# Maxima and exponentials that read a PSUM group in any order, with a newly searched instruction order, in linear attention followed by a squared-ReLU layer

## The chip, the core and the metric

The kernel runs on one core of a Trainium2 chip. Time is device time of one execution in microseconds. The engines are TensorE (PE, matrix products into PSUM), VectorE (DVE), ScalarE (ACT), GpSimd (POOL, here almost only an issuer of loads) and SyncE (SP, an issuer of stores and of transposes by DMA). All run their own queues in order, and wait for each other by semaphores.

## The reference

Eight batches of eight heads, 576 tokens, head width 64, 128 features. Attention is linear, with positive and negative exponential features; its output, 4608 tokens of 512, goes through a two-layer network with a squared ReLU between.

```python
def phi(x):
    proj = np.einsum('bhsd,df->bhsf', x, w_phi)
    proj = proj - np.max(np.abs(proj), axis=-1, keepdims=True)
    return np.concatenate([np.exp(proj), np.exp(-proj)], axis=-1)
q_p, k_p = (phi(q), phi(k))
kv = np.einsum('bhsf,bhsd->bhfd', k_p, v)
z = np.sum(k_p, axis=2)
num = np.einsum('bhsf,bhfd->bhsd', q_p, kv)
den = np.einsum('bhsf,bhf->bhs', q_p, z)[..., None] + 1e-06
...
h = np.maximum(x @ w_in, 0.0)
return (h * h @ w_out).astype(np.float32)
```

## The kernel before, in words

The kernel first lists some 1738 small operations in the order of the mathematics (`plan.add`), each with its engine, and then issues them in another order, written out by hand as the table `ORDER`. `pin` chains every instruction behind the previous one of its engine, so `ORDER` fixes each engine's queue. Waits between engines are made from what each instruction reads and writes. The costs and the read and write lists given to `add` belong to the search that made the tables; at run time nothing comes from them but the operation's number.

Five tables go with it. `ORDER` is the order of issue. `BASES` gives each PSUM group one of the eight banks. `STATES` chooses ACT or DVE for each operation that may run on either (relu, output copies, KV copies, copies of PE transposes). `GATES` names for every load of batches 2 to 7 an operation that must be over before POOL may issue it. `FILL` puts products of a zero tile into PE's queue in the first microseconds.

One batch of attention goes like this. Queries and keys are turned so that the head width lies on the partitions: by PE and a copy in batches 0 and 1 (L316), by a DMA that SP issues in batches 2 to 7 (L326: one for K, one for Q). A projection (Pk, Pq; L342, or L369 and L494 in the first batch) puts 128 tokens by 128 features for up to four tiles and two heads into two PSUM banks. From these the keys get a maximum of absolute values on DVE (Mk, L397) and two exponentials on ACT (Ekp, Ekn, L403), not yet scaled. The maxima go through an exponential (em, L416 and L422) and scale the values instead (V, L430 on DVE). KV (L458, L463) is the product of key features and scaled values, copied to bf16 by ACT or DVE (L190, L192). For the queries of batches 0 to 3 the maximum (L501) and the features (Fq L572, exponentials L587) come from two products; from batch 4 on ("turned") one product gives a maximum (Mq, L534) and two exponentials (L547), and a DMA turns the features (Xf, L551). The numerators and denominators come from NA and NB (L651), with a scaling between them (L663) and a division after (L673, L677); a DMA turns the result (Xx, L711) into the layer's input xT.

The layer works on 512 tokens at a time, nine such chunks. F1 (L797, four 128x512 matmuls) makes 128 hidden units, relu (L774 on ACT or L776 on DVE) and square (L783 on DVE) follow; F2 (L891, four matmuls at a time) sums over the hidden units; an output copy (ot, L190 or L192) and a store end it. Matmuls of the layer for earlier chunks stand in PE's queue between the small products of the next batch's attention. The first chunk runs in smaller pieces (L808, L822, L836) so as to start early.

Where one PSUM group is read by a maximum and by two exponentials, the listing of before has each of them as a reader and a writer of the group, in the order maximum, positive exponential, negative exponential; the negative one closes the group. The first batch's keys use one bank for each head of a pair, and there the two banks are taken in opposite order by the two engines.

Of the kernel before, what the change touches and what calls it, by code (L numbers as in the profile page):

```python
# [20 lines left out]
def act_cost(n):  # L21
    return max(n / 1200 + 0.050, 0.105), n / 1200 + 0.165 + SEM


def dve_cost(n):
    return n / 960 + 0.064, n / 960 + 0.150 + SEM
# [27 lines left out]
class Plan:  # L54
# [6 lines left out]
    def add(self, eng, cost, fn, r=(), w=(), opens=None, closes=None, dma=None, tiled=False, release=False, what=""):  # L61
        op = Op(eng, cost, fn, opens, closes, dma, tiled, release, len(self.ops), what)
        before = {}
# [44 lines left out]
def kernel(  # L108
# [13 lines left out]
    Fd = w_phi.shape[1]  # L122
# [181 lines left out]
    def attention(b):  # L304
# [49 lines left out]
        def kgroup_ops(g):  # L354
# [7 lines left out]
            if first:  # L362
# [11 lines left out]
                def maxes(e, last):  # L374
                    def fn():
                        pin(nc.vector.tensor_reduce(
                            out=mk_view(g)[:, e, :], in_=ps1(pj[e])[:, : n * Fd].rearrange("p (i f) -> p i f", f=Fd),
                            axis=AX.X, op=ALU.max, apply_absolute_value=True))
                    add("DVE", dve_cost(n * Fd), fn, r=[pj[e]], w=[pj[e], ("mk", s2, g, e)],
                        closes=pj[e] if last else None, what="Mk")  # L380

                def exps(e, last):
                    for sgn, dst, nm in ((1.0, kp, "kp"), (-1.0, kn, "kn")):
                        def fn(dst=dst, sgn=sgn):
                            pin(nc.scalar.activation(out=dst[slot][:, e, :n, :].rearrange("p i f -> p (i f)"),
                                                     in_=ps1(pj[e])[:, : n * Fd], func=ACT.Exp, scale=sgn))
                        add("ACT", act_cost(n * Fd), fn, r=[pj[e]], w=[pj[e], (nm, slot, e)],
                            closes=pj[e] if last and sgn < 0 else None, what="E" + nm)

                maxes(0, False)  # L390
                exps(1, False)
                exps(0, True)
                maxes(1, True)
# [6 lines left out]
            add("DVE", dve_cost(2 * n * Fd), fn, r=[pj], w=[pj] + [("mk", s2, g, e) for e in range(2)], what="Mk")  # L400
            for sgn, dst, nm in ((1.0, kp, "kp"), (-1.0, kn, "kn")):
                def fn(dst=dst, sgn=sgn):
                    pin(nc.scalar.activation(out=dst[slot][:, :, :n, :].rearrange("p e i f -> p e (i f)"),  # L403
                                             in_=ps2(pj)[:, :, : n * Fd], func=ACT.Exp, scale=sgn))
                add("ACT", act_cost(2 * n * Fd), fn, r=[pj], w=[pj] + [(nm, slot, e) for e in range(2)],
                    closes=pj if sgn < 0 else None, what="E" + nm)
# [117 lines left out]
        def q_turned(c):  # L524
# [12 lines left out]
            add("DVE", dve_cost(2 * n * Fd), fn, r=[pj], w=[pj, ("mq", s2, c)], what="Mq")  # L537
            for sgn, base in ((1.0, 0), (-1.0, 2 * n * P)):
# [9 lines left out]
                add("ACT", act_cost(2 * n * Fd), fn, r=[pj], w=[pj, ("qf", f, sgn)], closes=pj if sgn < 0 else None,  # L548
# [422 lines left out]
    0, 1, 14, 11, 10, 9, 13, 4, 5, 2, 7, 3, 6, 12, 20, 85, 74, 15, 86, 50, 75, 87, 51, 18, 76, 88, 89, 52, 41, 54,  # L971
    19, 77, 78, 17, 42, 55, 79, 53, 16, 58, 80, 82, 63, 90, 27, 64, 56, 93, 81, 29, 65, 57, 8, 21, 112, 61, 66, 67,
    108, 36, 62, 113, 83, 106, 91, 101, 25, 43, 109, 68, 100, 110, 44, 45, 28, 84, 111, 71, 22, 59, 46, 107, 102, 47,
    116, 49, 60, 94, 69, 99, 31, 147, 103, 48, 117, 72, 24, 148, 144, 23, 145, 119, 73, 92, 26, 149, 96, 228, 234,
    95, 98, 70, 172, 97, 30, 229, 126, 173, 120, 38, 122, 222, 127, 105, 32, 123, 230, 223, 121, 124, 104, 231, 128,
    37, 125, 235, 216, 130, 118, 129, 146, 175, 232, 131, 217, 137, 132, 39, 138, 176, 133, 139, 134, 210, 140, 211,
    135, 177, 141, 150, 136, 151, 158, 233, 161, 35, 159, 152, 162, 142, 329, 153, 143, 236, 160, 154, 163, 204, 330,
    237, 325, 33, 205, 164, 331, 155, 333, 257, 156, 238, 326, 157, 165, 206, 341, 327, 207, 239, 34, 328, 166, 344,
    167, 174, 342, 168, 114, 178, 332, 40, 115, 334, 179, 212, 378, 335, 337, 213, 345, 180, 202, 214, 181, 347, 182,
    203, 346, 215, 383, 186, 336, 169, 338, 187, 348, 183, 170, 339, 200, 184, 190, 171, 224, 241, 188, 340, 189,  # L980
    350, 191, 185, 225, 201, 379, 192, 267, 382, 356, 351, 245, 268, 385, 243, 256, 193, 357, 353, 194, 226, 218,
    343, 377, 195, 242, 219, 354, 362, 227, 505, 355, 247, 220, 196, 509, 197, 240, 269, 259, 221, 580, 264, 298,
    244, 246, 513, 394, 248, 352, 299, 265, 387, 208, 359, 249, 363, 381, 258, 300, 517, 585, 358, 380, 250, 209,
    280, 198, 251, 388, 281, 260, 518, 384, 254, 349, 386, 368, 364, 360, 199, 575, 282, 252, 361, 261, 262, 369,
    253, 255, 289, 370, 263, 276, 270, 290, 277, 365, 271, 395, 291, 292, 523, 293, 272, 366, 283, 374, 266, 284,
    294, 375, 285, 527, 286, 295, 287, 519, 307, 296, 273, 288, 308, 531, 301, 396, 309, 371, 302, 274, 316, 303,
    317, 535, 372, 304, 376, 318, 310, 305, 559, 275, 579, 279, 536, 311, 306, 581, 397, 401, 367, 312, 398, 541,
    537, 313, 399, 314, 297, 545, 419, 400, 373, 402, 278, 319, 582, 418, 315, 409, 549, 410, 403, 553, 417, 320,
    411, 563, 321, 393, 412, 567, 322, 554, 390, 420, 571, 404, 323, 578, 389, 444, 572, 466, 445, 450, 467, 576,
    510, 583, 451, 514, 511, 574, 441, 512, 515, 528, 421, 392, 468, 442, 506, 773, 529, 577, 457, 507, 413, 458,  # L990
    405, 777, 516, 502, 414, 584, 459, 524, 391, 503, 434, 778, 415, 520, 424, 406, 592, 532, 416, 530, 546, 508,
    425, 407, 427, 560, 423, 426, 504, 525, 422, 542, 547, 428, 533, 526, 593, 550, 521, 433, 543, 548, 408, 564,
    522, 534, 544, 447, 565, 435, 429, 586, 561, 448, 573, 538, 774, 430, 555, 551, 589, 324, 431, 552, 449, 446,
    452, 436, 475, 432, 484, 476, 610, 539, 439, 443, 437, 477, 440, 611, 568, 438, 460, 569, 556, 612, 461, 702,
    613, 540, 462, 706, 557, 772, 463, 570, 485, 566, 590, 602, 464, 756, 974, 486, 603, 465, 469, 775, 760, 470,
    971, 604, 558, 453, 587, 471, 454, 710, 771, 472, 562, 456, 605, 473, 493, 784, 714, 494, 474, 594, 598, 715,
    595, 764, 495, 716, 599, 617, 596, 768, 597, 478, 600, 776, 638, 479, 720, 591, 639, 601, 588, 480, 724, 782,
    481, 640, 616, 482, 654, 781, 487, 620, 655, 483, 496, 977, 488, 728, 769, 489, 623, 732, 615, 455, 490, 656,
    491, 738, 497, 622, 492, 625, 663, 641, 664, 498, 770, 642, 742, 789, 665, 746, 499, 624, 500, 606, 644, 619,
    750, 607, 501, 703, 751, 608, 739, 645, 631, 630, 969, 704, 699, 614, 621, 609, 980, 733, 721, 618, 780, 734,  # L1000
    705, 626, 700, 752, 722, 972, 717, 646, 701, 627, 973, 723, 632, 783, 740, 647, 672, 718, 799, 779, 673, 711,
    648, 970, 707, 674, 787, 800, 725, 708, 709, 628, 801, 712, 785, 735, 726, 713, 1168, 633, 790, 629, 757, 802,
    968, 719, 741, 636, 736, 758, 657, 637, 650, 727, 681, 651, 729, 682, 658, 634, 643, 730, 659, 747, 731, 683,
    635, 660, 761, 661, 748, 986, 666, 975, 791, 690, 667, 899, 691, 749, 737, 668, 903, 669, 692, 979, 792, 765,
    670, 793, 759, 649, 983, 794, 803, 662, 743, 766, 804, 978, 675, 671, 744, 753, 676, 812, 805, 745, 917, 1366,
    762, 754, 788, 677, 767, 813, 907, 806, 1166, 678, 763, 679, 684, 811, 653, 1362, 795, 685, 680, 847, 921, 786,
    755, 796, 1363, 925, 976, 848, 911, 820, 797, 686, 819, 929, 912, 821, 798, 687, 935, 688, 849, 689, 807, 835,
    930, 939, 836, 850, 943, 822, 837, 851, 947, 817, 808, 838, 693, 953, 948, 809, 957, 931, 840, 810, 913, 918,
    839, 652, 852, 908, 828, 694, 695, 909, 900, 910, 896, 696, 987, 901, 697, 827, 1167, 902, 871, 859, 919, 872,
    961, 897, 926, 816, 873, 920, 860, 936, 1176, 814, 874, 1178, 904, 898, 937, 861, 965, 815, 818, 927, 862, 823,  # L1010
    829, 914, 966, 863, 932, 905, 915, 824, 916, 988, 883, 922, 989, 933, 906, 990, 698, 940, 884, 923, 991, 825,
    924, 984, 967, 938, 954, 949, 981, 830, 826, 941, 841, 1008, 955, 958, 942, 842, 885, 833, 1011, 959, 843, 928,
    834, 831, 875, 886, 934, 950, 844, 889, 832, 864, 845, 1004, 951, 960, 853, 1005, 944, 982, 846, 1114, 945, 854,
# [100 lines left out]
```

## Time and profile before

| what | value |
|---|---|
| median of 3 runs | 354.33 us (352.88 to 354.97) |
| the profiled execution | 353.94 us |
| its span in the trace | 352.2 us |
| PE, DVE, ACT, POOL busy | 341.5, 268.9, 233.3, 96.2 us |
| first transposes on PE | 5.7 us after the span's start |
| granted TensorE clock | 0.995 of full speed, mean |

A page of a profile gives for each engine the time in which at least one of its instructions ran. Of a group of instructions it gives the line, the engine, the tiles written and read with their shapes, the count, busy time, the mean duration of one in ns, and the idle time of the engine ahead of them with what ended it ("<-DVE mk L397" means that an instruction of line 397 on DVE released it). A matmul's duration runs until its result is out, and the next one begins earlier than that.

### The profile page before, as it was taken

The numbers are of one execution on the slowest core, as the hardware profiler recorded it, in microseconds if no ns is written. First come the engines' busy times: TensorE is split into PE (matmuls) and PEld (weight loads), VectorE is DVE, ScalarE is ACT, GpSimd is POOL, SyncE is SP. The second block draws the span as 40 slices with busy tenths as digits, with TensorE's granted clock in tenths as the row PEclk, the third lists the DMA queues.
The fourth block names the chain that finished last, engine by engine and source line by source line (L and its number), as shares of the span: only waits on it lengthen the run. The fifth ranks groups of instructions, "written<-read, shape, count | busy, mean of one in ns | idle before, by whom it ended". The sixth has DMA issues, their size and how long they took to land.

```text
span 352.2 us, 8392 instructions
## 1 busy us (share of the span) xinstructions
PE 341.5 (97%) x3343; PEld 192.0 (55%) x3343; DVE 268.9 (76%) x513; ACT 233.3 (66%) x439; POOL 96.2 (27%) x144
## 2 busy tenths in 40 slices
PE   6999999999999999999999999999999999999995
PEld 6778866544644555445545555455555554444443
DVE  4899997889887989689979887877989653564150
ACT  3999997789885776976597785895596503212111
POOL 8673461282461636021421302040100000000000
PEclk9999999999999999999999999999999999999999
DMA  8999999999999899997999999999857431100115
GB/s 92 172 196 202 201 155 168 159 122 167 162 130 189 138 150 151 165 201 152 163 140 202 165 212 140 214 106 179 155 117 157 96 87 67 60 2 0 71 50 120
DMA packets 133623, 49.05 MB, mean 139 GB/s; under 512 B 102096, under 2 KB 129104, under 8 KB 133584
## 3 DMA queue, kind: packets, MB, share of 16 engines
q0 software_dynamic: 45232, 18.36, 46.0%
q1 hardware_dynamic: 88112, 29.99, 44.3%
q8 instruction: 26, 0.43, 0.5%
q10 hardware_dynamic: 240, 0.16, 0.2%
q14 instruction: 13, 0.11, 0.1%
HBM read 36.77 MB, written 9.44 MB: 131 GB/s over the span
## 4 chain that ended last, share of the span: by engine, by line
PE 77%; DVE 10%; ACT 5%; DMA 5%; issue 2%; SPq 0%; DVEq 0%; ACTq 0%; POOLq 0%
PE psum L797 27%; PE psum L891 27%; PE psum L651 4%; PE psum L458 4%; PE psum L342 4%; PE psum L836 2%; DMA out_dram<-ot 2%; DVE va L430 2%; DMA xT<-xo 2%; DVE mk L397 1%; ACT hr L774 1%; DMA xk<-in_k_dram 1%; DVE hr L776 1%; PE psum L572 1%; DVE h L783 1%
## 5 line engine op out<-in xcount | busy, mean ns | idle before, releaser
L891 PE MATMUL psum<-wout,h 128*128 128x512 bf16 x560 | 134.9, 379 | 0.2 <-ACT ot L192 0.2
L797 PE MATMUL psum<-xT,win 128*128 128x512 bf16 x448 | 106.9, 379 | 1.4 <-DVE hr L776 0.8
L774 ACT ACTIVATE hr<-psum 128x512 bf16<-128x512 f32 x103 | 59.8, 596 | 54.5 <-PE psum L797 36.8
L891 PEld LDWEIGHTS <-h 128*128 128x128 bf16 x560 | 50.4, 97 | 54.6 <-issue 0.9
L797 PEld LDWEIGHTS <-win 128*128 128x128 bf16 x512 | 47.6, 97 | 54.3 <-issue 2.7
L783 DVE TENSOR_TENSOR h<-hr 128x512 bf16<-128x512 bf16 x144 | 56.6, 415 | 20.6 <-ACT hr L774 19.8
L547 ACT ACTIVATE qf<-psum 128x1024 bf16<-128x1024 f32 (+1 forms) x40 | 36.5, 938 | 12.3 <-DVE mq L534 11.3
L397 DVE TENSOR_REDUCE mk<-psum 128x8 f32<-128x1024 f32 (+1 forms) x35 | 38.6, 1110 | 4.6 <-PE psum L342 4.5
L587 ACT ACTIVATE qpn<-psum 128x1024 bf16<-128x1024 f32 (+1 forms) x40 | 36.7, 938 | 5.7 <-PE psum L572 4.9
L403 ACT ACTIVATE kp<-psum 128x1024 bf16<-128x1024 f32 (+1 forms) x35 | 32.7, 935 | 9.3 <-DVE mk L397 9.2
L651 PEld LDWEIGHTS <-qpn 128*128 128x128 bf16 x624 | 27.8, 98 | 13.9 <-issue 1.0
L663 DVE TENSOR_TENSOR psum<-psum,en 128x520 f32<-128x520 f32 (+1 forms) x39 | 27.2, 701 | 9.5 <-PE psum L651 5.6
L776 DVE TENSOR_SCALAR hr<-psum 128x512 bf16<-128x512 f32 x41 | 27.8, 685 | 6.7 <-PE psum L797 6.2
L403 ACT ACTIVATE kn<-psum 128x1024 bf16<-128x1024 f32 (+1 forms) x35 | 32.8, 937 | 0.0
L651 PE MATMUL psum<-kv,qpn 128*128 128x65 bf16 x624 | 31.1, 193 | 0.0
L430 DVE TENSOR_TENSOR va<-xv,va 64x256 bf16<-64x256 bf16 (+2 forms) x66 | 30.1, 471 | 0.9 <-ACT va L422 0.2
L245 POOL DMA_DIRECT2D xv<-in_v_dram x27 | 19.7, 734 | 36.0 <-DVE h L783 11.8
L245 POOL DMA_DIRECT2D xk<-in_k_dram x28 | 20.6, 740 | 31.6 <-ACT va L422 20.0
L677 DVE TENSOR_TENSOR xo<-psum,rden 128x512 bf16<-128x512 f32 (+1 forms) x39 | 26.7, 686 | 1.4 <-DMA xT<-xo 0.7
L265 POOL DMA_DIRECT2D xq<-in_q_dram x24 | 17.4, 725 | 33.0 <-ACT hr L774 13.7
L534 DVE TENSOR_REDUCE mq<-psum 128x8 f32<-128x1024 f32 (+1 forms) x20 | 22.3, 1113 | 2.9 <-PE psum L342 2.7
L501 DVE TENSOR_REDUCE mq<-psum 128x8 f32<-128x1024 f32 (+1 forms) x20 | 22.0, 1111 | 0.9 <-PE psum L342 0.8
(79 smaller groups left out, 383.5 us busy)
## 6 DMA issues: line engine op xcount, KB each, us to landing
out_dram<-ot SPq DMA_DIRECT2D x32, 256.0 KB, 3.1
xk<-in_k_dram POOLq DMA_DIRECT2D x26, 128.0 KB, 4.6
xq<-in_q_dram POOLq DMA_DIRECT2D x24, 128.0 KB, 4.8
xv<-in_v_dram POOLq DMA_DIRECT2D x24, 128.0 KB, 4.5
win<-in_moe_w_in_dram POOLq DMA_DIRECT2D x4, 512.0 KB, 9.2
wout<-in_moe_w_out_dram POOLq DMA_DIRECT2D x4, 512.0 KB, 14.0
xq<-in_q_dram POOLq DMA_DIRECT2D x4, 256.0 KB, 7.1
out_dram<-ot SPq DMA_DIRECT2D x6, 128.0 KB, 2.4
```

The source lines that it names most:

```text
L245: pin(nc.gpsimd.dma_start(out=x[:, a * 512 : z * 512].rearrange("p (h x) -> p h x", x=4 * D), in_=src[b][2 * a : 2 * z, 0:512, :].rearrang ...
L397: pin(nc.vector.tensor_reduce(out=mk_view(g), in_=ps2(pj)[:, :, : n * Fd].rearrange("p e (i f) -> p e i f", f=Fd), axis=AX.X, op=ALU.max, ...
L403: pin(nc.scalar.activation(out=dst[slot][:, :, :n, :].rearrange("p e i f -> p e (i f)"), in_=ps2(pj)[:, :, : n * Fd], func=ACT.Exp, scale= ...
L430: pin(nc.vector.tensor_tensor(out=t[:, :, :D].rearrange("p m (x c) -> p m x c", c=2), in0=x.rearrange("p (m x c) -> p m x c", m=n, c=2), i ...
L547: pin(nc.scalar.activation(out=o, in_=i_, func=ACT.Exp, scale=sgn))
L587: pin(nc.scalar.activation(out=o, in_=i_, func=ACT.Exp, scale=sgn))
L651: pin(nc.tensor.matmul(out=o[:, u // 4, u % 4 * D1 : (u % 4 + 1) * D1], lhsT=qpn[slot][:, sg * half + u * m : sg * half + u * m + P], rhs= ...
L774: pin(nc.scalar.activation(out=hr[sl], in_=ps1(g), func=ACT.Relu))
L776: pin(nc.vector.tensor_scalar(out=hr[sl], in0=ps1(g), scalar1=0.0, scalar2=None, op0=ALU.max))
L783: pin(nc.vector.tensor_tensor(out=dst, in0=i_, in1=i_, op=ALU.mult))
L797: pin(nc.tensor.matmul(out=o, lhsT=win[mc // 4][:, kc, mc % 4 * P : (mc % 4 + 1) * P], rhs=x, start=(kc == 0), stop=(kc == KC - 1)))
L891: pin(nc.tensor.matmul(out=ps1(g), lhsT=h2[c % 2][mc // 4][:, mc % 4, tt * P : (tt + 1) * P], rhs=wout[mc // 4][:, mc % 4, :], start=(mc = ...
```

## The change

In the listing, the maximum and the two exponentials of a projection are now readers of its group only, so that the search may put them in any of the six orders; a mark (`lock`) tells the search that they exclude each other. The closing of the group is no longer tied to the negative exponential. Then all five tables are new. Every operation has the same number as before, does the same on the same data, and there are as many.

```diff
-    def add(self, eng, cost, fn, r=(), w=(), opens=None, closes=None, dma=None, tiled=False, release=False, what=""):
+    def add(self, eng, cost, fn, r=(), w=(), opens=None, closes=None, dma=None, tiled=False, release=False, what="", lock=None):
         op = Op(eng, cost, fn, opens, closes, dma, tiled, release, len(self.ops), what)
+        op.lock = lock
...
-            add("DVE", dve_cost(2 * n * Fd), fn, r=[pj], w=[pj] + [("mk", s2, g, e) for e in range(2)], what="Mk")
+            add("DVE", dve_cost(2 * n * Fd), fn, r=[pj], w=[("mk", s2, g, e) for e in range(2)], lock=pj, what="Mk")
...
-                add("ACT", act_cost(2 * n * Fd), fn, r=[pj], w=[pj] + [(nm, slot, e) for e in range(2)],
-                    closes=pj if sgn < 0 else None, what="E" + nm)
+                add("ACT", act_cost(2 * n * Fd), fn, r=[pj], w=[(nm, slot, e) for e in range(2)], lock=pj, what="E" + nm)
...
-            add("DVE", dve_cost(2 * n * Fd), fn, r=[pj], w=[pj, ("mq", s2, c)], what="Mq")
+            add("DVE", dve_cost(2 * n * Fd), fn, r=[pj], w=[("mq", s2, c)], lock=pj, what="Mq")
...
 FILL = {
-    85: (0, 26), 87: (0, 4), 63: (7, 27), 65: (7, 10), 112: (7, 4), 108: (7, 3), 110: (7, 3), 116: (7, 23),
-    147: (0, 5), 144: (3, 5), 228: (5, 2), 139: (7, 7), 135: (7, 4),
+    74: (0, 26), 76: (0, 6), 87: (0, 3), 52: (7, 26), 63: (7, 6), 65: (7, 6), 116: (7, 26), 112: (7, 25),
 }
```

What the tables change, counted from them:

| | before | after |
|---|---|---|
| groups (without the first batch's keys) with one maximum and two exponentials: maximum first, between, last | 55, 0, 0 | 26, 13, 16 |
| relu on ACT, on DVE | 103, 41 | 109, 35 |
| output copies on ACT, on DVE | 20, 15 | 24, 11 |
| KV copies on ACT, on DVE | 22, 10 | 20, 12 |
| filler products | 123 | 124 |
| POOL's first loads, ahead of the mask (ident) | k, k, k, k, k | k, k, k, k, q |
| instructions of ACT ahead of the first relu | 50 | 49 |

The next table is about the DMA that turns K or Q of a batch (`Xxk`, `Xxq`): the PE operations that stand in `ORDER` between it and the first projection that reads it, for some of the twelve.

| transpose | before | after |
|---|---|---|
| K of batch 2 | 7 F2 or F1 pieces, 4 NA, 3 NB, 1 Pq, 2 Fq | 6 F2 or F1 pieces, 2 NA, 2 NB, 1 Pq, 2 Fq |
| K of batch 4 | 7 F1 or F2, 1 KV, 1 Pk, 2 Pq, 1 Fq | 6 F1 or F2, 1 KV, 1 Pq, 1 NA, 1 NB |
| Q of batch 7 | 9 F1 or F2, 1 KV, 1 Pk, 1 Pq, 3 NA, 3 NB | 5 F2, 3 NA, 3 NB |

All 1738 numbers of `ORDER`, the 385 banks, the 231 choices and the 108 gates differ in most places and are left out here.

## What was predicted

> **What bounds the kernel now.** First the page's busy table and slices, to see which engine the span belongs to.
>
> ```profile
> PE 341.5 (97%) x3343; PEld 192.0 (55%) x3343; DVE 268.9 (76%) x513; ACT 233.3 (66%) x439; POOL 96.2 (27%) x144
> ...
> PE   6999999999999999999999999999999999999995
> ...
> DVE  4899997889887989689979887877989653564150
> ACT  3999997789885776976597785895596503212111
> ```
>
> TensorE (PE) is busy in 341.5 of 352.2 us, and VectorE (DVE) and ScalarE (ACT) are dense only up to about slice 31. Next the busy time of each engine in four stretches: two of the start, the mixed middle, and the tail of feed-forward matmuls.
>
> ```profile
> 10.00:20.00 10.00, 9.03 (x123) 6.74 (x122) 8.85 (x19) 9.48 (x25) 5.44 (x9) 0.98 1.52 183
> 20.00:30.00 10.00, 9.88 (x189) 7.98 (x189) 9.94 (x24) 10.00 (x19) 6.41 (x9) 1.00 1.37 199
> ...
> 28.00:275.00 247.00, 243.83 (x2575) 137.12 (x2574) 214.88 (x393) 194.17 (x360) 75.57 (x112) 1.00 1.08 162
> 275.00:340.00 65.00, 65.00 (x360) 30.46 (x359) 30.72 (x67) 15.24 (x30) 0.00 (x0) 1.00 0.20 56
> ```
>
> The columns after the length are PE, weight loads, DVE, ACT and POOL. From 10 to 30 us ACT (19.5 of 20) and DVE (18.8 of 20) are full: the first batch's features are limited by them. From 275 us on PE is busy without a gap. In the middle PE idles for 247 - 243.83 = 3.2 us. That understates what it loses, since a matmul counts as busy until its result is out, so a short stall hides behind the tail of the one before. I therefore count the matmuls of the middle and price each at its streaming rate. The counts:
>
> ```profile
> L891 PE MATMUL psum<-wout,h 128*128 128x512 bf16 x384 | 93.7, 380 | 0.2 <-ACT ot L192 0.2
> L797 PE MATMUL psum<-xT,win 128*128 128x512 bf16 x375 | 90.0, 379 | 1.4 <-DVE hr L776 0.8 <-DVE xo L677 0.4 <-ACT hr L774 0.3
> L651 PE MATMUL psum<-kv,qpn 128*128 128x65 bf16 x552 | 27.6, 193 | 0.0
> L458 PE MATMUL psum<-va,kp 128*128 128x65 bf16 x224 | 17.3, 193 | 0.0
> ...
> L342 PE MATMUL psum<-wphi,qT 64*128 64x128 bf16 x252 | 12.8, 218 | 0.6 <-DVE xo L677 0.5
> L342 PE MATMUL psum<-wphi,kT 64*128 64x128 bf16 x244 | 12.0, 218 | 0.3 <-ACT kn L403 0.3
> L836 PE MATMUL psum<-xT,win 128*128 128x256 bf16 x64 | 8.3, 273 | 0.2 <-ACT qT L192 0.2
> L572 PE MATMUL psum<-qT,wphi 64*128 64x512 bf16 (+1 forms) x34 | 6.3, 356 | 0.4 <-ACT qpn L587 0.4
> ```
>
> The rates are the distances between starts where nothing waits, from the chain and the timeline:
>
> ```profile
> 298.52 6.04 PE psum L797 x28
> ```
> ```profile
> 199.15 0.20 PE L458 MATMUL psum<-va,kp 128*128 128x65 bf16 x1
> ...
> 200.36 1.89 PE L797 MATMUL psum<-xT,win 128*128 128x512 bf16 x8
> ...
> 203.72 0.40 PE L651 MATMUL psum<-kv,qpn 128*128 128x65 bf16 x8
> 203.96 1.03 PE L797 MATMUL psum<-xT,win 128*128 128x512 bf16 x4
> ...
> 209.05 0.68 PE L342 MATMUL psum<-wphi,qT 64*128 64x128 bf16 x16
> 209.67 1.04 PE L891 MATMUL psum<-wout,h 128*128 128x512 bf16 x4
> ```
>
> A 512-wide matmul takes 6.04/28 = 0.216 us; eight output matmuls (L651) 203.96 - 203.72 = 0.24, 0.030 each; sixteen projections (L342) 0.62, 0.039 each; the two KV groups that begin at 199.15 take 1.21, so 0.60 for one. So the middle needs 759 x 0.216 = 163.9, 552 x 0.030 = 16.6, 28 KV groups (224/8) 16.8, 496 x 0.039 = 19.3, and 64 x 0.108 = 6.9 at half the 512-wide price. L572 I take at its full busy time, 6.3, and the groups not shown (first feed-forward pieces, transposes) at about 9, an estimate at a quarter of the 512-wide price each for 166 matmuls. Sum 238.8: some **8 us of stalls**, 3.2 of them visible as idle. This and nothing else can be won in the middle; the tail has none.
>
> By the Trainium skill ("Trainium Kernel Development and Optimization", Performance Expectations) matmul busy time is a bad measure of the distance to the limit, as matmuls are pipelined. Reading the busy column alone would put the ceiling of the gain at 3.2 us; by the count it is about 8.
>
> **The change part by part.** The programs issue the same work; only one filler matmul is added (124 for 123). What differs is order, banks, engines and the times at which loads may start.
>
> *Maxima and exponentials.* Past the first batch's K there are 55 groups with one maximum and two exponentials (35 of K, 20 of Q). In ORDER before, all 55 run the maximum first; afterwards 26 do, 13 have it between the exponentials and 16 last. Who waits now:
>
> ```profile
> ACT kp L403 <- DVE mk L397: 9.2, 11, 2.4
> ACT qf L547 <- DVE mq L534: 8.8, 8, 2.3
> ```
>
> So 18 us of ACT's 247 - 194.2 = 52.8 idle us in the middle stand behind a maximum. 29 of the 55 groups can spend that on an exponential instead. The price moves to DVE: where an exponential is first, the maximum waits for it, and behind it in DVE's queue wait the squares and the normalisations that PE needs. The reads themselves stay one after the other: the built program has a wait between engines in either order. The Trainium skill ("PSUM — Partial Sum Buffer", Terms) calls two engines on one bank at once a collision, two reads included, which speaks against any gain from reading together; by it only the order can win.
>
> What PE gets of it the trace of before can't show. Bounds: a gain of nothing, since PE waited for a K exponential only 0.3 us in the rows above, a gain of the whole 8 us, and on the other side a loss that the third rival below sets. I take 2.5, a third, nearer to the end at nothing, because that 0.3 is the nearest row.
>
> *Engines.* STATES moves, net, 6 relus and 4 output copies from DVE to ACT and 2 KV copies to DVE.
>
> ```profile
> L776 DVE TENSOR_SCALAR hr<-psum 128x512 bf16<-128x512 f32 x41 | 27.8, 685 | 6.7 <-PE psum L797 6.2
> L774 ACT ACTIVATE hr<-psum 128x512 bf16<-128x512 f32 x103 | 59.8, 596 | 54.5 <-PE psum L797 36.8
> L190 DVE COPY ot<-psum 128x512 f32<-128x512 f32 x15 | 10.2, 679 | 9.3 <-PE psum L891 9.1
> L192 ACT ACTIVATE ot<-psum 128x512 f32<-128x512 f32 x20 | 11.8, 594 | 16.0 <-PE psum L891 8.2 <-issue 6.7 <-DMA out_dram<-ot 1.0
> L190 DVE CAST kv<-psum 128x260 bf16<-128x260 f32 x10 | 4.3, 427 | 1.3 <-PE psum L463 1.3
> L192 ACT ACTIVATE kv<-psum 128x260 bf16<-128x260 f32 x22 | 8.4, 397 | 1.9 <-PE psum L463 1.8
> ```
>
> DVE: -6 x 0.685 - 4 x 0.679 + 2 x 0.427 = -6.0 us. ACT: 6 x 0.596 + 4 x 0.594 - 2 x 0.397 = +5.2 us. If all of it falls in the middle, DVE's idle there grows from 32.1 to 38.1 and ACT's shrinks from 52.8 to 47.6. PE's waits in the count above name DVE for 1.7 us and ACT for 1.4, so I share the 8 us as 4.4 and 3.6. If stalls go with the inverse of the idle time, DVE's 4.4 become 3.7 and ACT's 3.6 become 4.0: **-0.3 us**, an estimate, with bounds of -0.7 (ACT's growth hidden) and +0.4 (DVE's gain unused).
>
> *Start.* Counting each engine's queue up to the first relu (op 331), ACT has 49 instructions instead of 50, DVE as many as before up to the copies of the first x (56): nothing to gain where both are full. The first transposes need the first load and the mask (ident) that POOL makes:
>
> ```profile
> 3.33 1.46 POOL L245 DMA_DIRECT2D xk<-in_k_dram  x2
> ...
> 4.83 0.35 POOL L916 TENSOR_SCALAR_AFFINE_SELECT ident<-ident 128x128 bf16<-128x128 bf16 x1
> 5.07 1.83 POOL L274 DMA_DIRECT2D xq<-in_q_dram  x2
> ...
> 5.72 0.86 PE L316 MATMUL psum<-ident,xk 128*128 128x128 bf16 x10 [1.85 <-DMA xk<-in_k_dram]
> ```
>
> The mask stands behind five loads in both orders, but one of them is now a Q load of 1.83/2 = 0.92 us in place of a K load of 1.46/2 = 0.73. It is ready 0.2 us later, at about 5.4, still ahead of the load at 5.72. I take 0 for the start, between -0.6 and +0.6, one ACT instruction of 596 ns.
>
> *Transposes by DMA.* The one part that looks worse. K and Q of batches 2 to 7 are turned by a DMA that SP issues; from issue to landing:
>
> ```profile
> DMA to landing us min/median/max: 4.9/6.3/8.2
> ```
>
> Before, PE work standing between each of these twelve in ORDER and its first reader is never under 7.8 us: Q of batch 7 has 9 feed-forward groups of 4 x 0.216, 3 NA, 3 NB and smaller ones, 10.3. Afterwards that one has 5 feed-forward groups and 6 NA or NB of 0.24: 4.3 + 1.4 = **5.8**. The others that shrink are 6.6 (K of 4), 7.0 (K of 2), 7.2 (K of 7), 7.6 (Q of 3) and 7.6 (Q of 6). At the median landing only the first is late, by 0.5, and part of that lies beside stalls that are there anyhow; if all land at 8.2, the six cost 2.4 + 1.6 + 1.2 + 1.0 + 0.6 + 0.6 = 7.4. I take +0.5, by the median. SP's queue is in order, so a late transpose holds the ones behind it too; the nearest reader of a transposed output tile (xT) stands 6.0 us of PE work off, 5.8 before.
>
> *Loads.* The gates are all new, but the loads' work is the same and POOL idles for most of the middle (75.6 of 247 busy): 0, and if a load is late it shows as a late transpose, priced above.
>
> **Sum:** -2.5 - 0.3 + 0 + 0.5 = -2.3 us. The profiled execution took 353.94 us (span 352.2 and 1.7 around it), 0.1% under the median of the runs, 354.33. 353.94 - 2.3 = **351.6 us**, 0.8% under the median; by the bounds of the order's part this case reaches from 347.5 to 352.5.
>
> **Rivals.** *The stalls only move.* A stall is a handover that comes a little late, and a new order has handovers of its own. For it: PE's waits of the middle are spread over five of the lines counted above, none over 1.4 us in all, so no single cause can be taken away. Against it: the 18 us. Time: 353.9, between 352.6 and 356.1.
>
> *The transposes come late.* Mechanism: Q of 7, K of 4 and the four behind them; place: the first projection of a batch; price 7.4 at the longest landing. It decides from a landing of about 7.3 us on, where 1.5 + 0.7 + 0.3 + 0.1 = 2.6 eats the gain. For it: the longest measured is 8.2, and the DMA column of the stretches (the last but one) reads 1.08 in the middle against 0.20 in the tail, so the transposes never have the DMA engines to themselves. Against it: the median is 6.3. With no gain and landings of 8.2 in half of the cases: 353.9 + 3.7 = 357.6.
>
> ```profile
> L403 ACT ACTIVATE kp<-psum 128x1024 bf16<-128x1024 f32 (+1 forms) x35 | 32.7, 935 | 9.3 <-DVE mk L397 9.2
> ```
>
> *DVE waits for ACT.* 29 maxima now stand behind an exponential; if each held DVE's queue by a third of a full exponential (0.94 us in the row above), 8 us of DVE's 38 idle would go, and its 4.4 us of stalls would grow by the same rule to 5.6: +1.2, 355.1 without a gain. It lies inside the first rival and has its chance there.
>
> *It does nothing of what it says.* Excluded as far as the order goes: ORDER and the waits in the built program differ.
>
> **How the numbers follow.** Gain as forecast or more 0.48, stalls only move 0.30, late transposes (or what else ends above 356.1) 0.22. About 0.5%, 1.8 us, is what a measurement of this kernel can tell from no change, so faster is under 352.6, slower over 356.1. The range takes most of the gain's side (down to 347.5, where 6.4 of the 8 us would be gone) and of the slow side up to 358.0, leaving out a tenth at each end.
>
> **What would show it.** Right: in the profile after, ACT's idle behind L396 (maxima, one line up) is down from 9.2 to about 5, DVE busy falls to some 263, PE's busy in 28 to 275 us has the same matmuls plus some, and the tail begins about 2 us earlier. Wrong on the transposes: PE idle released by the DMA into kT or qT, or DMA rows in the chain before the projections (L343 there). Wrong on the order: DVE idle released by ACT's exponentials ahead of L396 and L532, of over 10 us, with PE waits on DVE grown.

## The result, and the profile after

The changed kernel takes 351.18 us (median of 8 runs, 349.62 to 352.78); the kernel before took 354.53 us in the same comparison (8 runs). The ratio is **0.9923, with a 95% interval of 0.9900 to 0.9947**. It compares the means of the fast executions, which leaves out one of the kernel before (359.51 us, in the slow state); of some 354 us it is a gain of 2.7 us, with 1.9 to 3.5 in the interval. The profiled execution took 350.52 us, its span 348.7 us, against 353.94 and 352.2 before: 3.4 to 3.5 us less. The forecast was 351.6 us. The total came out near the forecast, but it is a sum of other terms than those that I wrote, as the next sections show. What follows takes these two profiled executions apart, so its sums go to 3.5.

The busy table of the page and its slices, after:

```profile
PE 337.8 (97%) x3311; PEld 192.7 (55%) x3344; DVE 263.0 (75%) x505; ACT 237.6 (68%) x447; POOL 96.6 (28%) x144
...
PE   6999999999999999999999999999999999999994
...
DVE  3999898899988997798989897879787644653111
ACT  2999997699979879876986968787667312331310
```

DVE gave up 5.9 us and ACT gained 4.3 (6.0 and 5.2 were worked out). For PE the busy column can't be compared: 33 matmul records are missing from this trace (3311 of 3344), while the weight loads (PEld), of which every matmul has one, are complete. So I count the middle by weight loads. The same stretches of the middle and the tail (the third number from the end is the granted TensorE clock, 1.00 as before):

```profile
28.00:275.00 247.00, 245.00 (x2592) 140.44 (x2620) 212.02 (x391) 198.38 (x367) 77.00 (x113) 1.00 1.08 164
275.00:340.00 65.00, 64.74 (x339) 30.15 (x342) 27.80 (x63) 18.02 (x34) 0.00 (x0) 1.00 0.15 47
```

In the middle stand 2620 weight loads where before had 2574: 46 more products in the same 247 us. Which ones, says the view that groups the weight loads of this stretch by line. First before, then after; lines whose counts agree are left out:

```profile
L797 PEld LDWEIGHTS <-win 128*128 128x128 bf16 x376 | 34.4, 97 | 38.4 <-issue 2.6
L891 PEld LDWEIGHTS <-h 128*128 128x128 bf16 x384 | 33.6, 97 | 35.2 <-issue 0.9
L651 PEld LDWEIGHTS <-qpn 128*128 128x128 bf16 x552 | 24.6, 98 | 12.1 <-issue 1.0
...
L342 PEld LDWEIGHTS <-qT 64*128 64x128 bf16 x252 | 8.2, 94 | 8.3 <-issue 7.5
...
L572 PEld LDWEIGHTS <-wphi 64*128 64x128 bf16 x32 | 1.6, 93 | 3.5 <-issue 3.2
```
```profile
L889 PEld LDWEIGHTS <-h 128*128 128x128 bf16 x404 | 35.7, 97 | 38.4 <-issue 0.5 <-DVE h L781 0.4
L795 PEld LDWEIGHTS <-win 128*128 128x128 bf16 x373 | 34.2, 97 | 37.0 <-issue 0.6 <-DMA xT<-xo 0.2
L649 PEld LDWEIGHTS <-qpn 128*128 128x128 bf16 x568 | 25.5, 98 | 12.9 <-issue 0.4 <-ACT qpn L585 0.2
...
L343 PEld LDWEIGHTS <-qT 64*128 64x128 bf16 x256 | 8.0, 94 | 4.6 <-issue 3.0 <-DMA qT<-xq 0.4
...
L570 PEld LDWEIGHTS <-wphi 64*128 64x128 bf16 x34 | 1.7, 93 | 2.1 <-issue 1.9
...
L492 PEld LDWEIGHTS <-qT 64*128 64x128 bf16 x7 | 0.4, 94 | 0.4 <-issue 0.4
```

At the prediction's prices: 20 more F2 (+4.32 us), 3 fewer F1 (-0.65), 16 more output products (+0.48), 4 and 7 more projections (+0.43), 2 more of L570 at 6.3/34 each (+0.37). That is **4.95 us more work in the same time**: of the 8 us of stalls, an estimate, some 3 are left. The last two lines of this difference, nine products worth 0.6 us, are not new work: up to 28 us the changed kernel had done nine fewer of these (31 in place of 40). In the tail nothing was won: from 275 us to PE's last product 69.1 us remain in place of 73.6, and the products left there are 20 F2, 16 output products and 4 projections fewer and 2 F1 more, 4.5 us at the same prices.

What ACT and DVE wait for at the maxima and exponentials, in the view of waits from 28 to 275 us, after:

```profile
ACT kn L402 <- PE psum L343: 3.8, 4, 1.3
ACT qf L545 <- PE psum L343: 3.1, 2, 2.8
DVE mk L396 <- ACT kn L402: 2.3, 5, 0.7
DVE mq L532 <- ACT qf L545: 1.4, 4, 0.6
ACT kp L402 <- DVE mk L396: 0.7, 2, 0.4
ACT kn L402 <- DVE mk L396: 0.4, 1, 0.4
DVE mk L396 <- ACT kp L402: 0.2, 1, 0.2
```

ACT's 18 us behind maxima have become 0.7 + 0.4 = 1.1 us, and DVE now waits 2.3 + 1.4 + 0.2 = 3.9 us for exponentials, where the view of before has no such wait. ACT still waits at these places, but for PE; its idle time in all fell only from 52.8 to 247 - 198.4 = 48.6 us. The chain that ended last, by engine, after and (behind it) before:

```profile
PE 93%; DVE 3%; issue 1%; DMA 1%; ACT 1%; DVEq 0%; POOLq 0%
```
```profile
PE 77%; DVE 10%; ACT 5%; DMA 5%; issue 2%; SPq 0%; DVEq 0%; ACTq 0%; POOLq 0%
```

PE itself is now 93% of the chain. These shares are not amounts to win: 23% of before would be 81 us, and the count found some 8 us of stalls in the middle.

Two stretches look longer. At the start, the timeline's first exponential, after and before:

```profile
7.84 0.60 ACT L385 ACTIVATE kp<-psum 128x512 bf16<-128x512 f32 x1 [5.22 <-PE psum L370]
```
```profile
7.20 1.45 ACT L385 ACTIVATE kp<-psum 128x512 bf16<-128x512 f32 x3 [4.57 <-PE psum L369]
```

It begins 0.64 us later, and one instead of three run in a row. But this difference belongs to the two executions and not to the orders. PE ran its first products at two rates: a transpose took 0.104 us from start to start after (5.59 to 6.42 for eight) and 0.070 before (5.72 to 6.42 for ten), a filler 0.130 and 0.080, and the granted clock is shown as 1.00 from 5 to 7 us in both. Of the other runs below, three have the start of before and PE at the slower rate, and there the first exponential begins at 7.99 to 8.04 us (8.04 in the kernel with four output buffers); one has the start of after and PE at the faster rate, and it begins at 6.95:

```profile
6.95 1.23 ACT L389 ACTIVATE kp<-psum 128x512 bf16<-128x512 f32 x2 [4.31 <-PE psum L374]
```

At a like rate there is no such difference: 6.95 after against 7.15 and 7.20 at the faster one, and 7.84 to 8.18 after against 7.99 to 8.04 at the slower one. What the two profiled executions do differ by at the start is the nine products of above, 0.6 us. At the end, the timeline of the last matmuls, copies and stores, after:

```profile
340.46 3.66 PE L853 MATMUL psum<-wout,h 128*128 128x384 bf16 x32
340.52 3.90 SPq L904 DMA_DIRECT2D out_dram<-ot  x6
343.26 0.49 ACT L869 ACTIVATE otl<-psum 128x384 f32<-128x384 f32 x1 [5.41 <-PE psum L853]
...
344.51 1.39 SPq L876 DMA_DIRECT2D out_dram<-otl  x2
```

PE ends at 344.12, and the span 4.6 us later. Before, the last matmuls (L855) ran from 344.98 to 348.64, and the span ended 3.6 us behind them. After, SP still issues the stores of the chunk before (340.52 + 3.90 = 344.42) when the last copy is over (343.75). Against PE's end, SP's last stores begin 0.7 us later than before (344.51 - 344.12 and 348.30 - 348.64), and the span ends **1.0 us** later.

The account of the span of these two executions: -5.0 in the middle, +0.6 for the nine products of the start, +1.0 at the end, -3.4 in all; -3.5 was measured.

### The profile page after: what moved, and what is told of

Its sections match the earlier page's. It is cut to its first block, busy times and chain, and to the rows that moved or that the text cites. A ratio compares the mean times of both kernels' runs of the same rounds, so it can differ in the third digit from the quotient of the medians.

```text
span 348.7 us, 8370 instructions
## 1 busy us (share of the span) xinstructions
PE 337.8 (97%) x3311; PEld 192.7 (55%) x3344; DVE 263.0 (75%) x505; ACT 237.6 (68%) x447; POOL 96.6 (28%) x144
## 4 chain that ended last, share of the span: by engine, by line
PE 93%; DVE 3%; issue 1%; DMA 1%; ACT 1%; DVEq 0%; POOLq 0%
PE psum L889 35%; PE psum L795 32%; PE psum L649 5%; PE psum L343 5%; PE psum L456 5%; PE psum L834 2%; PE psum L317 1%; PE psum L570 1%; DMA xk<-in_k_dram 1%; PE psum L820 1%; PE psum L806 1%; PE psum L962 1%; PE psum L461 1%; PE psum L853 1%; DVE mq L499 1%
## 5 line engine op out<-in xcount | busy, mean ns | idle before, releaser
L889 PE MATMUL psum<-wout,h 128*128 128x512 bf16 x527 | 127.8, 380 | 2.1 <-issue 0.6
L795 PE MATMUL psum<-xT,win 128*128 128x512 bf16 x448 | 105.7, 379 | 0.1
L772 ACT ACTIVATE hr<-psum 128x512 bf16<-128x512 f32 x109 | 62.9, 599 | 54.6 <-PE psum L795 31.4
L795 PEld LDWEIGHTS <-win 128*128 128x128 bf16 x512 | 47.5, 97 | 52.8 <-issue 0.7
L396 DVE TENSOR_REDUCE mk<-psum 128x8 f32<-128x1024 f32 (+1 forms) x35 | 38.8, 1110 | 5.7 <-PE psum L343 3.0
L402 ACT ACTIVATE kn<-psum 128x1024 bf16<-128x1024 f32 (+1 forms) x35 | 32.8, 941 | 4.4 <-PE psum L343 3.8
L402 ACT ACTIVATE kp<-psum 128x1024 bf16<-128x1024 f32 (+1 forms) x35 | 32.7, 941 | 2.5 <-PE psum L343 1.5
L428 DVE TENSOR_TENSOR va<-xv,va 128x1024 bf16<-128x1024 bf16 (+2 forms) x66 | 30.5, 472 | 2.2 <-ACT va L420 1.5
L774 DVE TENSOR_SCALAR hr<-psum 128x512 bf16<-128x512 f32 x35 | 23.8, 682 | 7.5 <-PE psum L795 7.2
L246 POOL DMA_DIRECT2D xk<-in_k_dram x28 | 20.7, 749 | 25.1 <-DVE psum L661 13.2
L193 ACT ACTIVATE ot<-psum 128x512 f32<-128x512 f32 x24 | 14.3, 596 | 19.1 <-PE psum L889 19.1
L191 DVE COPY ot<-psum 128x512 f32<-128x512 f32 x11 | 7.5, 685 | 23.3 <-PE psum L889 18.6
L532 DVE TENSOR_REDUCE mq<-psum 128x8 f32<-128x1024 f32 (+1 forms) x20 | 22.1, 1111 | 2.1 <-ACT qf L545 1.4
```

The source lines that it names most:

```text
L246: pin(nc.gpsimd.dma_start(out=x[:, a * 512 : z * 512].rearrange("p (h x) -> p h x", x=4 * D), in_=src[b][2 * a : 2 * z, 0:512, :].rearrang ...
L396: pin(nc.vector.tensor_reduce(out=mk_view(g), in_=ps2(pj)[:, :, : n * Fd].rearrange("p e (i f) -> p e i f", f=Fd), axis=AX.X, op=ALU.max, ...
L428: pin(nc.vector.tensor_tensor(out=t[:, :, :D].rearrange("p m (x c) -> p m x c", c=2), in0=x.rearrange("p (m x c) -> p m x c", m=n, c=2), i ...
L772: pin(nc.scalar.activation(out=hr[sl], in_=ps1(g), func=ACT.Relu))
L795: pin(nc.tensor.matmul(out=o, lhsT=win[mc // 4][:, kc, mc % 4 * P : (mc % 4 + 1) * P], rhs=x, start=(kc == 0), stop=(kc == KC - 1)))
L889: pin(nc.tensor.matmul(out=ps1(g), lhsT=h2[c % 2][mc // 4][:, mc % 4, tt * P : (tt + 1) * P], rhs=wout[mc // 4][:, mc % 4, :], start=(mc = ...
```

## The experiments

All were timed in five rounds beside the kernel before, and ratios are to that kernel, which took 353.1 to 353.4 us there and 354.5 in the comparison above. So I compare a run with the changed kernel by their ratios, 0.9923 for the latter, and not by the difference of two times from two comparisons. Nothing of the computation is left out in any of them.

### The order of maximum and exponentials alone

In the changed kernel, every one of the 29 maxima that stand behind an exponential is put ahead of its group's first one; everything else stays:

```diff
-        return [self.ops[i] for i in ORDER]
+        order = list(ORDER)
+        for op in self.ops[200:]:
+            es = [o.seq for o in self.ops[op.seq + 1 : op.seq + 3] if o.what[:2] in ("Ek", "Eq")]
+            if op.what in ("Mk", "Mq") and len(es) == 2 and any(order.index(e) < order.index(op.seq) for e in es):
+                order.remove(op.seq)
+                order.insert(min(order.index(e) for e in es), op.seq)
+        return [self.ops[i] for i in order]
```

> The kernel after, all its tables kept, but in each of the 29 groups whose maximum stands behind an exponential the maximum is moved in ORDER to just ahead of the group's first exponential, as it was before. Theory (the freedom of order brings the gain): most of the 5 us that the middle won go, and the ratio to before comes back to 0.997 to 1.000 (353.5 to 354.5 us); ACT's idle time behind the maxima is back at 10 us or more. Rival (the new order as a whole brings it, and the place of a maximum is incidental): ratio 0.991 to 0.994 as for the kernel after, within 0.7 us.

In the kernel before, the reverse: the order within a group is made as it is afterwards where single moves can do it (22 of the 29 maxima behind an exponential, 29 pairs of exponentials exchanged), everything else stays:

```diff
+        for e in SWAPPED:
+            a, b = order.index(e), order.index(e + 1)
+            order[a], order[b] = order[b], order[a]
+        for m, e in BEHIND.items():
+            order.remove(m)
+            order.insert(order.index(e) + 1, m)
```

> The kernel before, all its tables kept, but 22 of the 29 groups have their maximum behind the exponential that it follows in the kernel after, and 29 pairs of exponentials are turned likewise (the other 7 groups can't be turned alone: there the maximum's own exponential stands ahead of the group's). Theory (the freedom by itself helps): ratio 0.993 to 0.998. Rival (it helps only with an order made for it): no gain, ratio 0.999 to 1.006, with DVE now waiting for ACT's exponentials in place of ACT for DVE.

Measured: 371.25 us, ratio 1.0517 [1.0495, 1.0539], and 372.64 us, 1.0540 [1.0517, 1.0563]. They lose 18 and 19.5 us against the kernel before, far more than any theory of mine gave. The middle stretch of the first, and its waits of ACT behind maxima (L402 and L538 are the maxima there, L408 and L551 the exponentials):

```profile
28.00:275.00 247.00, 230.93 (x2426) 130.17 (x2424) 197.18 (x361) 187.29 (x347) 77.04 (x113) 1.00 1.02 155
```
```profile
ACT qf L551 <- DVE mq L538: 15.4, 10, 4.1
ACT kn L408 <- DVE mk L402: 14.7, 10, 3.0
```

PE is busy 14 us less than after the change, and ACT stands 15.4 + 14.7 = 30 us behind maxima, more than the 18 of the kernel before. By the ratios, moving the 29 maxima in the finished order costs 1.0517 - 0.9923 = 5.9%, some 21 us or 0.7 us each. A moved maximum also passes other instructions in DVE's queue, two in the median and up to eight, so the edit changes more than the order within a group. In either direction the loss is much the same. What follows is that these edits don't measure what the freedom is worth. The reading that I hold is that they measure how closely each order is fitted: what stands behind a moved instruction comes late, and nothing in the order takes that up. That is argued, and not shown.

### The choice of engines alone

The table STATES of one kernel is put into the other; 98 of the 231 choices differ.

```diff
-    '0000000101100011110100100101100000000000000000010000000110000001100101100001100010000000000001001000'
...
+    '0000000101000111101000110010000000000000010000011100110000100010001000101001010001000010110010100010'
...
```

> The kernel after with the STATES of before: its order, but the old choice of DVE or ACT for relus and copies, which puts 6 us back on DVE. By the prediction's term the choice of engines is worth 0.3 us: ratio 0.992 to 0.994. Rival (each choice is tied to the order around it, so an unfit set costs more than its sum): ratio 0.997 or more.

> The kernel before with the STATES of after: 6 us less on DVE and 5 us more on ACT, in the old order. By the prediction's term: ratio 0.998 to 1.000. Rival (choices tied to the order): slower, ratio over 1.004.

Measured: the changed kernel with the old choices 360.60 us, 1.0203 [1.0183, 1.0223]; the kernel before with the new ones 362.35 us, 1.0250 [1.0228, 1.0273]. Both are slower than either kernel. The rival holds: the choices belong to their order. By their sums of busy time the new choices were to bring 0.3 us; exchanged alone, the old ones cost the changed kernel 1.0203 - 0.9923 = 2.8%, some 10 us, and the new ones cost the old kernel 2.5%, 9 us. So this table has no price whose sign turns with the direction of the exchange. The same holds for the places of the maxima above; the other tables were not exchanged.

### The end and the start

The stores of the chunk before the last (operations 1708 and 1709) are issued right behind operation 1707:

```diff
+        for s in (1709, 1708):
+            order.remove(s)
+            order.insert(order.index(1707) + 1, s)
```

> The kernel after, but the two stores of an output tile that is ready at 337.9 us move in SP's queue ahead of the two that wait for a tile ready at 340.5 us. In the kernel after six stores occupy SP from 340.5 to 344.4 us, 0.7 us past the end of the copy that the last stores need. Theory (SP's queue sets the end): 0.5 to 0.8 us faster than the kernel after, ratio to before about 0.990. Rival (the last landing is set by the last matmuls and the stores of the other queue): no change, ratio 0.992.

Nine fillers ahead of the first projections are left out, and one memset moves back:

```diff
+        order.remove(7)
+        order.insert(order.index(93) + 1, 7)
...
-    74: (0, 26), 76: (0, 6), 87: (0, 3), 52: (7, 26), 63: (7, 6), 65: (7, 6), 116: (7, 26), 112: (7, 25),
+    74: (0, 26), 52: (7, 26), 63: (7, 6), 65: (7, 6), 116: (7, 26), 112: (7, 25),
```

> The kernel after without the 9 filler products that stand ahead of the first two projections, and with a memset that isn't needed before batch 1 moved behind the sixth maximum. In the kernel after the first exponential begins at 7.84 us, in the kernel before at 7.20. Theory (the start lost 0.6 us there, and ACT, full from 10 to 30 us, hands it on to the end): 0.4 to 0.7 us faster than the kernel after, ratio about 0.991. Rival (the first loads or DVE's copies set the start anyway): no change, ratio 0.992.

And both together:

> The kernel after with both edits, of the start and of the last stores. If each does what its theory says, 0.9 to 1.5 us faster than the kernel after: ratio about 0.989. If neither does, 0.992.

Measured: 350.10 us, 0.9909 [0.9884, 0.9933]; 349.99 us, 0.9917 [0.9885, 0.9948]; both together 349.78 us, 0.9919 [0.9882, 0.9956]. In the first, the timeline shows that SP is free in time: the last store is issued when the copy (L873) is over.

```profile
338.35 5.42 SPq L908 DMA_DIRECT2D out_dram<-ot  x6
...
343.73 0.49 ACT L873 ACTIVATE otl<-psum 128x384 f32<-128x384 f32 x1 [5.41 <-PE psum L857]
344.25 1.17 SPq L880 DMA_DIRECT2D out_dram<-otl  x2
```

There the span ends 4.2 us behind PE's end at 344.59, 0.4 less than in the changed kernel; PE ends 0.5 later, and the span is 348.8 us, as long as before the edit (348.7). In the second, with PE at the slower rate of the changed kernel's execution (a transpose 0.103 us), the first exponential begins at 7.40 us, where it began at 7.84, and two run in a row:

```profile
7.40 1.08 ACT L388 ACTIVATE kp<-psum 128x512 bf16<-128x512 f32 x2 [4.77 <-PE psum L373]
```

So both edits do in the trace what was expected of them, at the end for 0.4 of the 1.0 us. But the intervals of all three ratios cover 0.9923. Whether any of these versions is faster than the changed kernel, these runs can't tell.

### The times of the loads

The gates of the changed kernel are taken away, so that a load of batches 2 to 7 waits only for its own buffer:

```diff
-GATES = {
-    377: 80, 378: 183, 379: 356, 380: 205, 381: 343, 382: 103, 383: 240, 384: 208, 385: 151, 386: 343, 387: 168,
...
-}
+GATES = {}
```

> The kernel after with no gates: POOL issues each load as soon as its buffer is free. It shows what the times of the loads are worth. Theory (the loads' work is the same, and early loads harm nothing): ratio 0.991 to 0.994. Rival (early loads run beside the transposes, and these land later than the measured 4.6 to 6.5 us, with PE waiting for turned K and Q): 2 us or more slower than the kernel after, ratio 0.998 or more.

Measured: 358.89 us, 1.0159 [1.0121, 1.0197], 1.0159 - 0.9923 = 2.4% or some 8 us over the changed kernel. The rival holds: when loads go matters by 2%, with the same bytes. The transposes of K and Q (L327), from issue to landing, first in the changed kernel and then without gates:

```profile
DMA to landing us min/median/max: 4.6/6.1/6.5
```
```profile
DMA to landing us min/median/max: 4.6/5.9/12.8
```

And what PE waits for in the middle without gates:

```profile
PE psum L795 <- DMA xT<-xo: 3.7, 3, 1.9
PE psum L889 <- ACT ot L193: 2.1, 1, 2.1
PE psum L795 <- ACT hr L772: 1.0, 1, 1.0
```

The median transpose is as fast as with gates, and the slowest takes twice as long. The largest wait is that of F1 for its transposed input (xT), which SP issues too; these transposes landed in 2.8 us in the median in both, and the slowest in 11.5 us in place of 7.2. So without gates some transposes on which PE depends land late. That they run beside an early load is the likely reason; which load met which transpose stays open.

### The freedom with everything else fitted to it

Since nothing can be undone alone, I searched ORDER (from its 261st place on) and STATES again, replaying the instructions with the durations and landings measured in the traces; banks, gates and start stay. Three searches of the same length: the changed kernel with free order within a group, the changed kernel with the maximum first in all 55 groups (there the table differs from place 214 on), and the kernel before with the maximum first. The first table differs like this, and the others in the same manner:

```diff
-    ... 218, 189, 240, 193, 357, 353, 194, 227, 343, 362,
+    218, 189, 246, 357, 343, 193, 194, 240, 379, 391, ...
...
```

> Control: ORDER (from its 261st place on) and STATES of the kernel after are searched once more by moves of single operations, with a replay of the queues at durations and landings measured in the two traces; banks, gates and the start are kept, and maxima and exponentials may stand in any order. Both theories: about as the kernel after, ratio to before 0.988 to 0.996.

> The same search, as long, from the same kernel, but under the old rule: in all 55 groups the maximum stands ahead of both exponentials. Theory (the freedom of order is worth the gain): it can't get back to the kernel after, and ends at 0.997 or more, at least 1.5 us behind the control. Rival (the freedom is worth nothing once the order is made for the rule; the 5 per cent of the first experiment were the price of moving operations out of a finished order): within 0.003 of the control, 0.988 to 0.997.

> The same search, as long, from the kernel before, with its banks, gates and start, under the old rule. If an order made for the measured landings is what the change brings, this gets most of the gain without the freedom: ratio 0.990 to 0.996. If the gain needs the freedom or the new banks and gates: 0.998 or more.

Measured: 361.74 us, 1.0224 [1.0183, 1.0264]; 365.37 us, 1.0327 [1.0300, 1.0353]; 355.49 us, 1.0063 [1.0038, 1.0087]. All three lose, the first of them 3.0%, 10.6 us, against the tables that it began from; what I expected of it was wrong. With the control lost, the third, which lies above the 0.998 of its expectation, says nothing of what the gain needs. In the first one, the landings of the K and Q transposes and PE's longest waits:

```profile
DMA to landing us min/median/max: 4.6/5.9/13.2
```
```profile
PE psum L343 <- DMA kT<-xk: 4.4, 1, 4.4
PE psum L795 <- DMA xT<-xo: 2.5, 2, 1.3
```

My replay took a landing as a fixed time, but here the longest is 13.2 us where the changed kernel had 6.5. So the search's landings did not hold on the chip; that it moved transposes and loads to where they meet is the likely reason, not shown. With the maximum first, the same search is 1.0327 - 1.0224 = 1.0% (3.6 us) worse, and ACT stands 12.2 + 8.8 + 6.2 us behind maxima again, where the first search has 4.5 in all:

```profile
ACT qf L545 <- DVE mq L532: 12.2, 7, 4.1
ACT kn L402 <- DVE mk L396: 8.8, 6, 2.6
ACT kp L402 <- DVE mk L396: 6.2, 5, 3.8
```

That points to a worth of the freedom of about 1%, but it is one search of each kind, both kernels are far from the changed one, and their waits for DMAs differ as well. How much of the 3.4 us is the freedom, and how much a better search with measured landings, **stays open**.

### A fourth output buffer in the kernel before

The kernel before had 1.0 us of ACT's idle time behind a store (L192 in the prediction's rows). Its chain shows that store as one of its longest pieces, and a transpose of an output tile as another:

```profile
65.90 5.67 DMA xT<-xo
...
101.09 6.66 DMA out_dram<-ot
```

A fourth output tile takes the wait away without touching the order:

```diff
+    ot.append(otl)
...
-            sl = oslot[0] % 3
+            sl = oslot[0] % 4
```

> The kernel before with a fourth output buffer (the one that otherwise only the last tile uses), nothing else. In its trace one output copy stands 1.0 us behind a store that took 6.7 us to land, and holds ACT's queue. Theory (late landings that the old order had no room for cost it part of the 5 us): 0.5 to 1.2 us faster, ratio 0.9965 to 0.9985. Rival (the wait is absorbed before PE feels it): 0.999 to 1.001.

Measured: 352.51 us, 0.9977 [0.9964, 0.9989], so 0.8 us less. The theory holds, and the wait is gone from the output copies on ACT in the middle, whose four copies into the fourth tile (otl) wait for nothing either:

```profile
L193 ACT ACTIVATE ot<-psum 128x512 f32<-128x512 f32 x9 | 5.3, 592 | 0.1
```

The waits of before name no other copy that stood behind a store. The changed kernel keeps three tiles and has no ACT wait for a store either (its output copies wait 19.1 us, all for PE). So an amount of 0.8 us, a quarter to a third of the gain, can be had without any freedom of the maxima; that the new order has it for this reason was argued from the missing wait, and not tried. Nor was the other piece: after the change, the chain has no DMA in the middle at all, and the transposes of output tiles (L711, L709 after) landed in 2.8 us in the median where before they took 4.0. That a part of the gain comes from there is a rival that no run here tests.

## Why the prediction was right, and where its terms were not

- **What bounds the kernel: right.** The stalls of the middle were the thing to win, the count put them at 8 us and the busy column at 3.2. The change won 5.0 us there, more than the busy column had. Counting against streaming rates was what made a range down to 347.5 possible. That 347.5 to 352.5 follow "by the bounds of the order's part" is wrong, though: bounds of 8 us and of nothing give 353.94 - 8 + 0.2 = 346.1 and 354.1 with the other terms as they stand.
- **Order of maxima and exponentials, -2.5: the sign held, the size was too small.** I took a third of 8 us, because PE's visible wait for a K exponential was only 0.3. With all five tables, the middle gained 5.0. The sign to look for was there, and stronger: ACT's idle time of K exponentials behind maxima (L396) fell from 9.2 to 0.7 + 0.4 = 1.1 us, where about 5 had been given, and that of Q's from 8.8 to nothing that the view shows. That the gain comes from the order within the groups alone wasn't shown.
- **Engines, -0.3: the step itself failed.** It priced a choice by its engine's sum of idle time. The runs with exchanged tables cost 9 to 10 us in both directions. The sum of busy times came out well (263.0 for a forecast of some 263), but it says nothing of the price.
- **Transposes, +0.5: didn't come.** The longest landing was 6.5 us where before it was 8.2, and the waits of the middle name one of these twelve once, with 0.4 us. The shorter stretch of PE work ahead of a projection was there; that the new gates kept other loads away is what the 12.8 us without gates suggest. I had taken the landings of before as fixed, which is also the error of my own search.
- **Loads, 0: right only with the gates as they are.** Without them the kernel is some 8 us slower. The sentence that the gates are free because POOL idles looked at the issuing engine, and not at what the loads meet.
- **Start, 0 within 0.6: about right.** In the two profiled executions nine products are late by 28 us, 0.6 us. The first exponential, 0.64 us later there, comes at much the same time where PE runs at a like rate. I had counted instructions in the queues of ACT, DVE and POOL, and not the fillers in PE's queue: six stand ahead of the first projection, where before had four. Nor had I asked at what rate PE runs there.
- **Tail, nothing: wrong by 1.0 us.** I had read that PE has no gap there, and stopped at PE. What stands behind PE's end, SP's queue with the stores of the chunk before, I had not looked at.
- **Rivals.** That the stalls only move does not fit the 46 further products, nor a ratio whose interval ends at 0.9947. Late transposes don't fit the landings. DVE's wait for ACT came true at 3.9 us (10 was the limit given), and the middle has no wait of PE of over 0.5 us for DVE. Its price was worked out wrongly: 29 x 0.94 / 3 is 9.1 us and not 8, and the rule then gives +1.4 and not +1.2.

The sum -2.3 was near the -3.4 of the profiled runs, and the 2.7 of the ratio, since a gain in the middle twice as large as given was offset by 1.6 us at both ends, in places that I had set to nothing. So it was forecast rightly that stalls of the middle would go, and the closeness of the total is in good part luck.

## What to carry to other kernels

In an order that a search has fitted, a part may have no price of its own: here both directions of each exchange lost 9 to 21 us. So don't read the worth of a part from undoing it alone, and predict the sum by the stalls that are left to win. Count these by products and streaming rates, not by busy time, and then look separately at what happens ahead of the first product and behind the last one. Where a schedule rests on DMA landings, its loads' times belong to it: the slowest of the same twelve transposes landed in 6.5 us with the gates and in 12.8 without. And before a difference at the start is put down to an edit, look whether two executions with the same start agree.

## What the hardware showed that I had not expected

A projection (eight products of 64 rows) takes different times by what follows it. The timeline of the changed kernel:

```profile
135.45 0.40 PE L343 MATMUL psum<-wphi,kT 64*128 64x128 bf16 x8
135.69 0.39 PE L343 MATMUL psum<-wphi,qT 64*128 64x128 bf16 x8
136.01 0.82 PE L889 MATMUL psum<-wout,h 128*128 128x512 bf16 x3
```

Ahead of another projection it takes 135.69 - 135.45 = 0.24 us, ahead of a product of 128 rows 136.01 - 135.69 = 0.32. In the middle of both kernels it takes 0.22 to 0.24 us ahead of products of 64 rows (26 places) and, but for three, 0.31 to 0.34 ahead of products of 128. By the Trainium skill ("TensorEngine Tiling (Array Packing)", Key Properties) a change of the tiling mode drains TensorE; the rows agree, at some 0.08 us here. Counted from ORDER, PE goes from 64-row to 128-row products 60 times before and 57 times after: at 0.1 us each that is some 0.3 us, an estimate, of the middle's gain, which my count put under stalls.

The second is that PE's first products ran at one of two rates, at a granted clock shown as 1.00: the same eight transposes took 0.83 us in one execution (5.59 to 6.42) and 0.46 in another with the same start (5.60 to 6.06, in the run with the stores moved). In the profile of before, the granted clock is then 0.50 from 8 to 10 us.

The third is the spread of DMA times: transposes of one shape, issued by the same queue, landed within 4.6 to 6.5 us in one kernel and 4.6 to 13.2 us in another, at nearly the same median (6.1 and 5.9).
